# Two fp32 products in one kernel: where and when the sums of the weights' blocks are formed, split and stored in chunks 0 and 1

## The chip, the cores and the metric

The kernel runs on one core of a Trainium2 chip. The metric is the device time of one execution in microseconds. TensorE (PE) multiplies, VectorE (DVE) and GpSimd (POOL) do the element-wise work on two operands, ScalarE (ACT) the casts and the GELU. SyncE (SP) issues most DMAs in one fixed order, so that a DMA which has to wait for its data holds up every later one of that queue; a smaller queue of DMAs is issued by POOL between its own instructions.

## The reference

What the kernel computes, with 8 batches × 8 heads × 576 positions × 64:

```python
kv  = einsum('bhsd,bhse->bhde', k, v)
out = einsum('bhsd,bhde->bhse', q, kv)
rms = sqrt(mean(out * out, axis=-1, keepdims=True) + 1e-06)
x   = (out / rms * g_norm).transpose(0, 2, 1, 3).reshape(4608, 512)
h   = x @ w_in                              # 512 x 2048
g   = 0.5 * h * (1 + erf(h / sqrt(2)))
return (g @ w_out).astype(float32)          # 2048 x 512
```

## The kernel before, in words

The 4608 rows of `x` are worked in 9 chunks (`NCH`) of 512. To keep fp32 accuracy, each operand is held as a high half (a cast on ACT) and a low half (operand minus high half, on DVE), and a product of two operands is three matmuls: high·high, low·high, high·low. Between the two layers of a chunk the kernel forms the rows of the next chunk: `load_kv` and `sum_kv` for the keys and values, `scale` for the norm, `add_blocks` for sums of blocks.

**Chunk 0** is plain while the weights arrive. For each of the 16 blocks `i`, `layer1` (12 matmuls of 128x512) and `layer2` of block `i-1` (12 more) run, and `convert` turns the raw weights of two or three tiles into halves: `bits_w` (DVE, the `SCALAR_TENSOR_TENSOR` rows of L682), the low halves (DVE L695). The GELU's low half is `gl` (DVE L730). `bits_w` writes into two places, `x4` and `x5`, in turn.

**Chunk 1** (`FAST`) has a plain layer 1, and its layer 2 takes 7 block products in place of 8. It is worked in 28 steps, "ticks", of 12 matmuls of 128x256. Each tick's operand is made four ticks ahead by `ready` (high half ACT L1171, low half DVE L1172) from tiles that `combine` (L1161) adds up. **Chunks 2 to 8** do so in both layers.

The 7 products need sums of blocks of the weights, and these are formed once:

- `w_in` has eight pairs of tiles `j`. `sum_in(j)` adds four 128x256 blocks on DVE in chunk 0 (L581). For pairs 0 to 4 the sums go to DRAM from POOL's queue; in chunk 1 `load_sums` (SP L482) brings half a pair back, `high_sums` (ACT L487) and `low_sums` (DVE L491) split it, and `send(rounded)` has `product_out` (SP L417) write two 256 KB blocks to DRAM. For pairs 5 to 7 (`DIRECT = 5`), `split_in` does it at once in chunk 0: ACT casts into `x4` and `x5` (L429), DVE subtracts (L430), and POOL issues eight DMAs of 128 KB a pair out of those tiles (L437).
- `w_out`'s pairs: `sum_out(j)` does two 128x512 adds on DVE into `z`, then four 128x256 adds on POOL from `z` to `w` (L581 both). `split_out(j)` (ACT L995, DVE L996) writes the halves over the weights' own tiles, and `send(sent)` stores them.

The raw weights of chunk 1's layer 2 come by `load_raw` (SP L1025), and its first three, for the first ticks, stand at the end of layer 1 in SP's order. SBUF places that fall free are listed in `free` and handed out by `take`; the tile of weight `i` (`w_in{i}`) falls free when `layer1` has used it. In chunks 2 to 8 the sums come in through a ring of six tiles (`fetch`), but for those that stay (`RESIDENT`, `IN_PLACE`).

In chunk 1's layer 1 two PSUM banks (`h`) take the results in turn; ACT L1344 reads each. What stands behind it in an iteration is in this order:

```python
if i in SPLITS:
    split_out(SPLITS[i])
if i in SUMS_OUT:
    sum_out(SUMS_OUT[i])
```

Of the kernel before, what the change touches and what calls it, by code (L numbers as in the profile page):

```python
# [36 lines left out]
def linear_attn_rms_gelu_ffn(  # L37
# [371 lines left out]
    def product_out(at, src, eng=nc.sync):  # L409

        key, n = at[:-1], at[-1]
        if key in RAW_KEPT:
            to = resident_tile(key)[:, n * DM:(n + 1) * DM].rearrange("p (a n) -> p a n", a=2)
            eng.dma_start(out=to.bitcast(F32), in_=src.bitcast(F32))
            return
        to = product_of(key)[:, n * DM:(n + 1) * DM]
        eng.dma_start(out=to.rearrange("p (a n) -> p a n", a=2), in_=src.bitcast(F32))  # L417

    def product_of(key):
        if key not in products:  # L420
# [68 lines left out]
    def low_sums(j, second):  # L489
# [4 lines left out]
        t = t.rearrange("p (z k n) -> p k z n", z=2, k=2)  # L494
        rounded.extend(
            (place_in(j, k), t[:, a]) for a, k in enumerate((6, 5) if second else (1, 2))
        )
        rounded.append(name)
# [35 lines left out]
    def fetch(n):  # L534

        if n < len(queue):
# [938 lines left out]
```

## Time and profile before

| | |
|---|---|
| median of three runs | 799.0 us (798.01 to 800.65) |
| the profiled execution | 799.7 us, of which the span of instructions is 797.9 us |
| PE busy | 770.0 us (97% of the span) |
| DVE, ACT, POOL busy | 579.8, 392.6, 192.5 us |
| DMA | 253.84 MB, mean 318 GB/s |

Busy time is an average over all nine chunks; it says that PE has the most work, not where it stands still. In the rows below a piece such as `[6.65 <-DMA x]` is the idle time ahead of an instruction and what ended it; times are microseconds from the start of the span, and L numbers are those of the kernel before.

### The profile page before, as it was taken

The page shows a single profiled execution, that of the slowest core. Times are in us where ns is not written, and L with a number is a line of the kernel's source. Part 1 is how long each engine was busy: PE and PEld are TensorE (multiplying, and loading weights), DVE is VectorE, ACT ScalarE, POOL GpSimd, SP SyncE. Part 2 cuts the span into 40 slices and gives each one's busy share as a digit, 9 for nine tenths or more (in the row PEclk, how much of TensorE's full clock was granted, in tenths as well). Part 3 has the DMA queues.
Part 4 walks back from the last instruction along what each step waited for, and adds up shares of the span by engine and source line. Part 5 has one row for each costly group of instructions (what it writes and reads, how often), then busy time and mean ns, then how long its engine had stood idle before and what let it go on. Part 6 is the DMA issues. An engine that isn't in the chain of part 4 may idle for free.

```text
span 797.9 us, 17145 instructions
## 1 busy us (share of the span) xinstructions
PE 770.0 (97%) x6728; PEld 732.5 (92%) x6728; DVE 579.8 (73%) x1022; ACT 392.6 (49%) x760; POOL 192.5 (24%) x189
## 2 busy tenths in 40 slices
PE   9999599985999999999999999999999999999998
PEld 7888388764999999999999999999999999999998
DVE  3986676675965897589748974798489758975683
ACT  3997655642534453445444543454445444542361
POOL 1012323367101710071007200620071007101200
PEclk9999799997999999999999999999999999999999
DMA  9999987968699999799979997998899899789974
GB/s 348 407 413 400 370 281 259 314 201 277 208 307 348 336 350 406 259 332 358 406 266 330 345 399 283 326 337 301 295 330 333 297 314 324 277 279 362 327 277 143
DMA packets 98228, 253.84 MB, mean 318 GB/s; under 512 B 9572, under 2 KB 43876, under 8 KB 98148
## 3 DMA queue, kind: packets, MB, share of 16 engines
q1 hardware_dynamic: 96160, 246.98, 86.3%
q0 software_dynamic: 1984, 5.77, 1.9%
q8 instruction: 53, 0.87, 0.4%
q14 instruction: 27, 0.22, 0.1%
q10 hardware_dynamic: 4, 0.00, 0.0%
HBM read 214.43 MB, written 36.70 MB: 315 GB/s over the span
## 4 chain that ended last, share of the span: by engine, by line
PE 81%; ACT 6%; DMA 4%; DVE 3%; issue 3%; POOL 2%; SPq 0%; DVEq 0%; POOLq 0%; ACTq 0%
PE acc L1193 27%; PE acc L590 21%; PE h L590 13%; PE a L1193 11%; PE h L715 4%; PE acc L738 2%; ACT z L658 1%; POOL w L581 1%; PE acc L183 1%; ACT r L671 1%; DMA w_out<-w_out 1%; DMA w_in<-qT 1%; PE acc L237 1%; PE a L237 1%; DMA products_in<-x 1%
## 5 line engine op out<-in xcount | busy, mean ns | idle before, releaser
L590 PE MATMUL acc<-w_out,w_in 128*128 128x256 f32 x660 | 87.6, 276 | 0.0
L590 PEld LDWEIGHTS acc<-w_out,w_in 128*128 128x128 f32 x660 | 80.7, 188 | 0.0
L715 PE MATMUL h<-x,w_in 128*128 128x512 f32 x276 | 73.5, 392 | 0.0
L715 PEld LDWEIGHTS h<-x,w_in 128*128 128x128 f32 x276 | 51.6, 188 | 11.6 <-issue 0.6
L1193 PE MATMUL acc<-w_in,w_out 128*128 128x256 f32 x468 | 58.3, 276 | 0.0
L1193 PEld LDWEIGHTS acc<-w_in,w_out 128*128 128x128 f32 x468 | 55.5, 188 | 0.0
L590 PE MATMUL h<-w_out,w_in 128*128 128x256 f32 x396 | 53.6, 277 | 0.0
L1193 PE MATMUL acc<-w_in,w_in 128*128 128x256 f32 x408 | 50.7, 276 | 0.0
L590 PEld LDWEIGHTS h<-w_out,w_in 128*128 128x128 f32 x396 | 48.9, 188 | 0.5 <-issue 0.4
L1193 PEld LDWEIGHTS acc<-w_in,w_in 128*128 128x128 f32 x408 | 48.3, 188 | 0.0
L581 DVE TENSOR_TENSOR gl<-acc,gh 128x256 f32<-128x256 f32 (+1 forms) x78 | 34.7, 444 | 18.6 <-ACT gh L603 14.0
L738 PE MATMUL acc<-w_out,gh 128*128 128x512 f32 x128 | 42.9, 418 | 3.4 <-ACT gh L724 3.4
L590 PE MATMUL acc<-w_in,w_in 128*128 128x256 f32 x300 | 41.8, 276 | 0.0
L269 ACT ACTIVATE sq<-acc 128x512 f32<-128x512 f32 x14 | 8.4, 603 | 65.4 <-PE acc L237 65.4
L590 PEld LDWEIGHTS acc<-w_in,w_in 128*128 128x128 f32 x300 | 37.6, 188 | 0.0
L590 PE MATMUL acc<-s,w_in 128*128 128x256 f32 x270 | 37.1, 276 | 0.0
L279 DVE TRANSPOSE_TENSOR_REDUCE part<-sq 128x16 f32<-128x512 f32 x33 | 23.3, 707 | 17.8 <-ACT sq L269 17.8
L622 ACT ACTIVATE w_out<-acc 128x512 f32<-128x512 f32 x33 | 19.8, 599 | 33.4 <-DVE acc L581 33.4
L1193 PE MATMUL acc<-w_out,w_in 128*128 128x256 f32 x282 | 35.6, 278 | 0.0
L738 PEld LDWEIGHTS acc<-w_out,gh 128*128 128x128 f32 x128 | 25.8, 203 | 9.8 <-ACT gh L724 4.3
L715 PE MATMUL h<-s,w_in 128*128 128x512 f32 x96 | 30.2, 396 | 4.4 <-ACT w_in L1344 2.9
L1193 PEld LDWEIGHTS acc<-w_out,w_in 128*128 128x128 f32 x282 | 33.9, 188 | 0.1
(362 smaller groups left out, 1966.9 us busy)
## 6 DMA issues: line engine op xcount, KB each, us to landing
w_in<-products_in SPq DMA_DIRECT2D x172, 512.0 KB, 5.2
w_in<-products_out SPq DMA_DIRECT2D x142, 512.0 KB, 5.4
products_in<-w_in SPq DMA_DIRECT2D x42, 256.0 KB, 5.7
products_out<-w_out SPq DMA_DIRECT2D x38, 256.0 KB, 5.1
w_in<-w_in SPq DMA_DIRECT2D x16, 512.0 KB, 11.6
w_out<-w_out SPq DMA_DIRECT2D x16, 512.0 KB, 11.3
q<-qT SPq DMA_DIRECT2D x15, 512.0 KB, 7.1
kv_main<-kv_main SPq DMA_DIRECT2D x14, 512.0 KB, 8.3
```

The source lines that it names most:

```text
L183: nc.tensor.matmul(out=ps[r, n * D:(n + 1) * D], lhsT=k[:, r], rhs=v[:, r], start=(j == 0), stop=(j == NJ),)
L237: nc.tensor.matmul(out=ps[rows(h), p % 2 * HALF + a:p % 2 * HALF + e], lhsT=kv[b % 2][rows(half), p, h ^ half], rhs=q[rows(half), h, a:e], ...
L269: nc.scalar.activation(out=sq, in_=ps, func=AF.Square)
L279: nc.vector.tensor_reduce(out=self.part[:, 2 * k[0] + k[1], :], in_=sq.rearrange("p (b d) -> p b d", d=BLK), op=ALU.add, axis=AX.X, apply_ ...
L581: return eng.tensor_tensor(out=out, in0=x, in1=y, op=op)
L590: nc.tensor.matmul(out=out, lhsT=y, rhs=x[:, z, kb], start=first and kb + i == 0, stop=kb == 1 and i == 2, skip_group_check=True,)
L622: nc.scalar.activation(out=grid(t)[:, :, j % 2], in_=ps.rearrange("p (a n) -> p a n", a=2), func=AF.Gelu)
L658: nc.scalar.activation(out=zs[n].bitcast(F32), in_=top.bitcast(F32), func=AF.Prelu, scale=2.0 ** -112, alpha=2.0 ** 32,)
L671: nc.scalar.activation(out=tails[n], in_=raw[n].bitcast(mybir.dt.uint8).rearrange("p (n b) -> p n b", b=8)[:, :, 3], func=AF.Copy, scale=1 ...
L715: nc.tensor.matmul(out=h, lhsT=parts["in", i][:, w][:, p * P:(p + 1) * P], rhs=at.x[p][:, x], start=(m + p == 0), stop=(m == 2 and p == NP ...
L738: nc.tensor.matmul(out=ps, lhsT=x[:, ts], rhs=parts["out", i][:, w], start=(i == 0 and m == 0), stop=(m == 2 and (i == NF - 1 or (i, t) == ...
L1193: nc.tensor.matmul(out=self.bank[name][a][:, a * HALF:(a + 1) * HALF], lhsT=x[:, at], rhs=y, start=(k in (0, 2, 1) and n + p + m == 0 and ...
```

## The change

1. `split_in`, `DIRECT` and `pending` are gone. All eight pairs of `w_in` send their sums to DRAM in chunk 0, and the halves of pairs 5 to 7 are loaded, split and written in chunk 1: 11 halves in layer 1 (`LOAD`, split three iterations after the load, before two), five in layer 2 (`LATE`, split four ticks after).
2. `sum_out` adds in place, in one pair of tiles (`SPOTS`) in place of two. Pairs 0 to 3 are summed in chunk 0 (`SUMS_0`), two of them split there (`SPLITS_0`); pairs 4 to 7 follow in chunk 1.
3. `layer1` in chunk 1 uses four PSUM banks in turn: `h0`, `h1`, `acc0`, `acc1`.
4. Chunk 0's `scale` moves from DVE to POOL, one of its `split_x` from POOL to DVE. Chunk 1's `scale` uses the work tiles `gh`, `gl`, not a place of `free`.
5. `load_kv(3, ...)`'s last two stand at iterations 8 and 10 (before 10 and 12), `raw_out(6)` and `(7)` at 5 and 6 (before both at 0). `take` hands out the place that has been free longest. The four resident loads are spread over chunk 2's start (`KEEP`), and of `w_out`'s sums (6,2) stays in place of (1,2).

```diff
-    pending = []
-    def split_in(j, s, first):
-        for t, hi in zip(s, first):
-            nc.scalar.copy(out=hi.bitcast(F32R), in_=t)
-            nc.vector.tensor_tensor(
-                out=t.bitcast(F32R), in0=t, in1=hi, op=ALU.subtract
-            )
-        for z, parts_z in enumerate((first, s)):
-            for n, k in enumerate((1, 2, 6, 5)):
...
-                nc.gpsimd.dma_start(
-                    out=to, in_=parts_z[n // 2][:, n % 2 * HALF:(n % 2 + 1) * HALF]
-                )
-    DIRECT = 5
...
-        if direct:
-            pending.append((j, s, (a, b)))
-            return
...
     def load_sums(j, second):
-        name, t = take(F32R, first=SHORT)
+        n = 2 * j + second
+        if n < len(KEPT_RAW):
+            name, t = KEPT_RAW[n], block_tile(KEPT_RAW[n], F32R)[:, :2 * DM]
+        else:
+            name, t = take(F32R, first=RINGS if n >= LATE[3] else SHORT)
...
-    IN_PLACE = [(k, GROUPS - 1) for k in (1, 2, 6, 5)] + [(1, 2), (2, 2)]
+    IN_PLACE = [(k, GROUPS - 1) for k in (1, 2, 6, 5)] + [(2, 2), (6, 2)]
...
-        name = next(n for n in [*(n for n in first if n in free), *free]
+        name = next(n for n in [*(n for n in free if n in first), *free]
...
-        h = next_bank("h")
+        h = bank(f"acc{i % 2}") if at.c and i % 4 > 1 else next_bank("h")
...
-            if 12 <= i < 15:
-                for n in ((0,), (1, 2), (3,))[i - 12]:
-                    nxt.scale(n)
+            if 11 <= i < 15:
+                nxt.scale(i - 11, nc.gpsimd)
             if i in (13, 14):
-                nxt.split_x(i - 13)
+                nxt.split_x(i - 13, nc.vector if i == 13 else nc.gpsimd)
...
-    halves = [(j, second) for j in range(DIRECT) for second in range(2)]
+    halves = [(j, second) for j in range(NJ2) for second in range(2)]
...
+    SPOTS = {0: "x5", 1: "x5", 2: "w", 3: "z", 4: "w", 5: "z", 6: "w", 7: "z"}
-    def sum_out(j):
+    def sum_out(j, eng=nc.gpsimd):
...
-        for o, x, op, y in (
-            (s1, a21, ALU.add, a22), (s2, s1, ALU.subtract, a11),
-            (s3, a11, ALU.subtract, a21), (s4, a12, ALU.subtract, s2),
-        ):
-            add(o, x, y, op, nc.gpsimd)
-        wide[j] = s
+        add(a22, a21, a22, eng=eng)
+        add(a21, a11, a21, ALU.subtract, eng)
+        add(a11, a22, a11, ALU.subtract, eng)
+        add(a12, a12, a11, ALU.subtract, eng)
+        wide[j] = w
...
+    SUMS_0 = {12: 0, 13: 1, 14: 2, 15: 3}
+    SPLITS_0 = {13: 0, 14: 1}
...
+                send(rounded)
+                if i in LATE:
+                    load_sums(*halves[LATE[i]])
+                if i - 4 in LATE:
+                    high_sums(*halves[LATE[i - 4]])
+                    low_sums(*halves[LATE[i - 4]])
...
-    SUMS_OUT = {0: 1, 2: 2, 4: 3, 5: 4, 7: 5, 9: 6, 11: 7}
-    SPLITS = {0: 0, 2: 1, 4: 2, 5: 3, 7: 4, 9: 5, 11: 6, 13: 7}
-    LOAD = {1: 1, 2: 2, 4: 3, 5: 4, 6: 5, 8: 6, 9: 7, 11: 8, 12: 9}
+    SUMS_OUT = {1: 4, 3: 5, 5: 6, 7: 7}
+    SPLITS = {0: 2, 1: 3, 3: 4, 5: 5, 7: 6, 9: 7}
+    LOAD = {-1: 0, 0: 1, 1: 2, 2: 3, 3: 4, 4: 5, 5: 6, 6: 7, 7: 8, 9: 9, 11: 10}
+    LATE = {3: 11, 5: 12, 7: 13, 9: 14, 11: 15}
+    KEEP = {(0, False): (0, 1), (2, False): (2,), (4, False): (3,)}
...
-        if i in (10, 12):
-            load_kv(3, i // 2 - 3)
+        if i in (8, 10):
+            load_kv(3, i // 2 - 2)
```

DVE's order in chunk 0, around block `i = 7` (`x5_415` and `x4_454` are the two places `x5`, `x4`; `w_908`, `w_909` the sums of pair 5). Before:

```order
L581 TENSOR_TENSOR w_909<-x5_415,w_908 128x256
L682 SCALAR_TENSOR_TENSOR x5_415<-z_903,r0_336 128x512
L730 TENSOR_TENSOR gl_950<-h1_936,gh_949 128x512
L695 TENSOR_TENSOR w_in11_953<-x4_454,w_in11_953 128x512
L430 TENSOR_TENSOR w_908<-w_908,x5_415 128x512
L430 TENSOR_TENSOR w_909<-w_909,x4_454 128x512
L682 SCALAR_TENSOR_TENSOR x5_415<-z_955,r0_336 128x512
L695 TENSOR_TENSOR w_out10_977<-x5_415,w_out10_977 128x512
```

and of the change, whose L567, L668, L716 and L681 are the L581, L682, L730 and L695 of before:

```order
L567 TENSOR_TENSOR w_909<-x5_415,w_908 128x256
L668 SCALAR_TENSOR_TENSOR x5_415<-z_903,r0_336 128x512
L716 TENSOR_TENSOR gl_954<-h1_940,gh_953 128x512
L681 TENSOR_TENSOR w_in11_957<-x4_454,w_in11_957 128x512
L668 SCALAR_TENSOR_TENSOR x5_415<-z_959,r0_336 128x512
L681 TENSOR_TENSOR w_out10_965<-x5_415,w_out10_965 128x512
```

The two L430 are gone, and the next write to `x5` no longer stands behind a cast and four DMAs that read it. The same holds for the two later pairs.

SP's order at the end of chunk 1's layer 1. Before (`sums_4_1` is the second half of pair 4, the last that is loaded):

```order
L482 DMA w_in11_1976<-sums_4_1_821 128x512
L137 DMA w_in7_1978<-kv_main 128x1024
L159 DMA w_in8_1915<-kv_tail 128x256
L1025 DMA w_in12_1981<-products_out_0_0_782 128x1024
L1025 DMA w_in13_2008<-products_out_0_1_930 128x1024
L417 DMA products_in_4_0_1233<-w_in10_1952 128x2x256
L417 DMA products_in_4_1_1237<-w_in10_1952 128x2x256
L1025 DMA w_in14_2033<-products_out_0_2_1106 128x1024
```

and of the change (L470, L1008, L426 are L482, L1025, L417 of before):

```order
L137 DMA w_in9_1904<-kv_main 128x1024
L159 DMA w_in3_1848<-kv_tail 128x256
L426 DMA products_in_4_0_1216<-w_in6_1823 128x2x256
L426 DMA products_in_4_1_1220<-w_in6_1823 128x2x256
L470 DMA w_in10_1926<-sums_5_0_914 128x512
L1008 DMA w_in6_1950<-products_out_0_0_782 128x1024
L426 DMA products_in_2_3_1965<-w_in8_1878 128x2x256
L426 DMA products_in_4_2_1218<-w_in8_1878 128x2x256
L1008 DMA w_in12_1974<-products_out_0_1_934 128x1024
L1008 DMA w_in8_1997<-products_out_0_2_1082 128x1024
```

The kv loads now stand ahead of pair 4's last writes. Two of the three raw loads (L1008) go into `w_in6` and `w_in8`, out of which the two writes just ahead of each still read.

POOL's order from chunk 0's end on. Before, behind the 24 L437 (the first four rows are the last of those; then chunk 0's `split_x`, then `sum_out(0)` of chunk 1):

```order
L437 DMA products_in_0_1267<-w 128x256
L437 DMA products_in_1_1269<-w 128x256
L437 DMA products_in_3_1081<-w 128x256
L437 DMA products_in_2_1272<-w 128x256
L348 TENSOR_TENSOR s_1363<-o,s_1363 128x512
L348 TENSOR_TENSOR s_1413<-o,s_1413 128x512
L581 TENSOR_TENSOR w<-z 128x256
L581 TENSOR_TENSOR w<-w,z 128x256
```

and of the change, where the first six rows stand in chunk 0:

```order
L330 TENSOR_TENSOR o<-o,sq 128x512 x2
L567 TENSOR_TENSOR x_415<-x_415 128x256 x4
L330 TENSOR_TENSOR o<-o,sq 128x512
L567 TENSOR_TENSOR x_415<-x_415 128x256 x4
L330 TENSOR_TENSOR o<-o,sq 128x512
L348 TENSOR_TENSOR s_1400<-o,s_1400 128x512
L567 TENSOR_TENSOR w<-w 128x256 x4
L567 TENSOR_TENSOR z<-z 128x256 x4
```

In place of DMA issues POOL has four `scale` and two `sum_out` in chunk 0; six `sum_out` follow, in `w` and `z` in turn.

## Rows read from the trace of the kernel before

**Rows 1.** Waits of PE: line, what it waited for, us in total, times, longest.

```profile
PE acc L183 <- DMA w_in<-kv_main: 6.6, 1, 6.6
PE acc L738 <- DVE gl L730: 6.0, 1, 6.0
PE acc L738 <- ACT gh L724: 3.4, 1, 3.4
PE h L715 <- ACT w_in L1344: 2.9, 2, 1.7
PE h L715 <- ACT s L1344: 1.5, 1, 1.5
```

**Rows 2.** Windows by stage: stretch, length, busy PE, PEld, DVE, ACT, POOL, clock, DMA share, GB/s.

```profile
60.00:77.40 17.40, 17.40 (x96) 14.21 (x95) 12.40 (x24) 14.71 (x27) 4.85 (x9) 1.00 1.05 401
77.40:103.30 25.90, 16.51 (x50) 11.89 (x49) 15.87 (x29) 16.23 (x32) 7.01 (x13) 0.74 1.04 361
103.30:127.90 24.60, 24.60 (x177) 20.17 (x176) 19.67 (x36) 11.42 (x22) 6.90 (x10) 1.00 0.76 257
127.90:182.10 54.20, 49.80 (x255) 39.43 (x253) 37.52 (x56) 27.37 (x52) 28.08 (x32) 1.00 0.78 254
182.10:202.60 20.50, 11.54 (x117) 10.36 (x117) 12.26 (x12) 7.07 (x14) 16.86 (x14) 0.67 0.84 285
202.60:237.80 35.20, 35.20 (x306) 34.94 (x304) 28.09 (x46) 17.14 (x31) 0.00 (x0) 1.00 0.80 275
237.80:797.90 560.10, 556.79 (x5281) 553.21 (x5280) 410.36 (x736) 252.07 (x496) 123.15 (x90) 1.00 0.89 319
```

**Rows 3.** Timeline of chunk 0's stall: start, us, engine, line, operation, idle time before.

```profile
80.63 0.69 DVE L682 SCALAR_TENSOR_TENSOR x<-z,r 128x512 int32<-128x512 int32 x1 [6.65 <-DMA products_in<-x]
...
97.57 0.69 DVE L682 SCALAR_TENSOR_TENSOR x<-z,r 128x512 int32<-128x512 int32 x1 [5.16 <-DMA products_in<-x]
```

**Rows 4.** Chain that ended last, 77 to 128 us: start, us, what.

```profile
108.73 2.48 PE a L183 x80
...
116.95 2.74 PE h L715 x12
119.70 2.80 PE acc L738 x12
```

**Rows 5.** DMA issues: tile, queue, count, KB each, us from issue to landing.

```profile
w_in<-sums SPq DMA_DIRECT2D x9, 256.0 KB, 3.5
...
products_in<-x POOLq DMA_DIRECT2D x12, 128.0 KB, 6.7
```

**Rows 6.** Timeline of layer 2's start in chunk 1, 176 to 206 us.

```profile
195.86 0.62 ACT L1171 CAST w_in<-s 128x512 fp32r<-128x512 f32 x1 [6.77 <-DMA products_in<-w_in]
```

**Rows 7.** SP's queue: waits of 100 to 240 us, as in rows 1.

```profile
SPq L159 <- POOL o L330: 8.2, 1, 8.2
```

**Rows 8.** Window inside chunk 1's layer 2, columns as in rows 2.

```profile
204.00:216.00 12.00, 12.00 (x107) 12.00 (x106) 11.96 (x21) 7.18 (x14) 0.00 (x0) 1.00 0.65 238
```

**Rows 9.** Chain that ended last, 180 to 240 us: a write of sums, and one tick.

```profile
193.87 4.88 DMA products_in<-w_in
...
205.80 1.37 PE a L1193 x12
```

**Rows 10.** Timeline of POOL and DVE in chunk 1, 104 to 206 us.

```profile
129.94 0.73 POOL L581 TENSOR_TENSOR w<-z 128x256 f32<-128x256 f32 x1 [6.70 <-DVE z L581]
...
175.16 5.46 POOL L330 TENSOR_TENSOR o<-o,w_in 128x512 f32<-128x512 f32 x4
...
183.15 0.73 POOL L581 TENSOR_TENSOR w<-z 128x256 f32<-128x256 f32 x1 [2.52 <-DVE z L581]
...
190.01 1.75 DVE L1172 TENSOR_TENSOR w_in<-x,w_in 128x512 fp32r<-128x512 f32 x1
...
203.41 0.68 DVE L1172 TENSOR_TENSOR w_in<-w_in,w_in 128x512 fp32r<-128x512 f32 x1
```

More of the change, by code (lines that the diff above doesn't have):

```diff
@@ L400, in linear_attn_rms_gelu_ffn, with product_of, product_of_key @@
     products = {}
+    def product_of(key):
+        if key not in products:
+            products[key] = dram.tile([P, 2, DM], F32, name="_".join(map(str, ("products", *key))))
+        return products[key]
+    def product_of_key(key):
+        return product_of(key).rearrange("p a n -> p (a n)")
     def resident_tile(key):
@@ L493, in low_sums @@
         )
[L494 to L498, printed above, removed]
+        rounded.append(([place_in(j, k) for k in ((6, 5) if second else (1, 2))], by_place(t)))
+        if name not in KEPT_RAW:
+            rounded.append(name)
     ORDER = (0, 2, 4, 6, 1, 3, 5)
@@ L543, in fetch @@
             ring[n] = kept[i][:, away:away + 2 * DM]
-            nc.sync.dma_start(out=ring[n].bitcast(F32), in_=products[key])
+            nc.sync.dma_start(out=ring[n].bitcast(F32), in_=product_of_key(key))
     def aligned(c, key):
@@ L1021, in load_raw @@
         away = AWAY if k == 3 else 0
-        name = next(x for x in [*first, *SHORT, *free] if x in free)
+        name = next(x for x in [*first, *(x for x in free if x in SHORT), *free] if x in free)
         free.remove(name)
         t = block_tile(name, F32R)[:, away:away + 2 * DM]
-        nc.sync.dma_start(out=t.bitcast(F32), in_=products["out", k, n])
+        nc.sync.dma_start(out=t.bitcast(F32), in_=product_of_key(("out", k, n)))
         raws[FAST, k, n] = name, t
@@ L1045, in op_tile @@
         shifted = n == GROUPS - 1 or k == 3 or (k, n) in IN_PLACE
-        names = [x for x in (SHORT if i < 17 else KEPT_IN) if x in free]
+        names = [x for x in free if x in RINGS and i < 17] + [x for x in free if x in KEPT_IN]
         if shifted or not names:
-            return take(F32R, True)
+            return take(F32R, i >= 17, [x for x in PLACES if x not in SHORT])
         free.remove(names[0])
@@ L1128, in linear_attn_rms_gelu_ffn @@
             load_w(BEHIND[i])
+        if i in SPLITS_0:
+            split_out(SPLITS_0[i])
+        if i in SUMS_0:
+            sum_out(SUMS_0[i])
         if i == 15:
@@ L1131, in linear_attn_rms_gelu_ffn @@
             load_sums(*halves[0])
-            sum_out(0)
+            send(sent)
     class Fast:
@@ L1370, in linear_attn_rms_gelu_ffn @@
         if i in (9, 10):
-            if i == 9:
-                names["spread"], spread = take(first=SHORT)
-            for n in range(2):
-                nxt.scale(
-                    (0, 2, 1, 3)[2 * (i - 9) + n], nc.gpsimd, spread[:, n * CH:(n + 1) * CH]
-                )
-            if i == 10:
-                free.append(names.pop("spread"))
+            for n, name in enumerate(("gh", "gl")):
+                spread = work.tile([P, CH], F32, name=name, bufs=2)
+                nxt.scale((0, 2, 1, 3)[2 * (i - 9) + n], nc.gpsimd, spread)
         if i in (11, 12):
@@ L1407, in linear_attn_rms_gelu_ffn @@
         before_layer1(c)
-        if c == FAST + 1:
-            for key in RESIDENT[:NJ2 // 2]:
-                keep(key)
         for j, second in parts_of_layer1():
+            if c == FAST + 1:
+                for n in KEEP.get((j, second), ()):
+                    keep(RESIDENT[n])
             if not second:
```

82 lines of the change are left out of this document (34 added, 48 removed).

## The prediction

> **What bounds the kernel now.** I read the waits of PE first [rows 1]: there are few, and they are long. The windows by stage then say where they fall [rows 2]. Chunks 2 to 8, the last of the windows, keep PE busy for 556.79 of 560.10 us: nothing to gain there. The loss stands in three places ahead of them.
>
> *Chunk 0, 77.4 to 103.3 us.* The window is 25.90 us long and holds 50 matmuls, two blocks' worth. A block at full pace takes 2.74 + 2.80 us [rows 4], so two take 11.1, and 14.8 us are lost: PE waits 3.4 and 6.0 us for the GELU's halves [rows 1], and the rest is shorter idle time and a clock of 0.74 in that window. The reason is one step further back. DVE stands 6.65 and 5.16 us ahead of a `bits_w` [rows 3], since the place that it writes is still read by POOL's DMAs of `split_in`, which take 6.7 us to land [rows 5]. DVE's queue is in order, so `gl` waits behind it.
>
> *Chunk 1's layer 1.* PE waits 2.9 + 1.5 = 4.4 us for ACT to read a result bank [rows 1]. PE is busy 49.80 of 54.20 us, which agrees.
>
> *The start of chunk 1's layer 2, 182.1 to 202.6 us.* The window of 20.5 us holds 117 matmuls: the 80 of a kv sum (2.48 us [rows 4]) and three ticks (1.37 us each [rows 9]), 6.6 us of work. So 13.9 are lost. SP's queue had stood for 8.2 us with a load of the keys' tail, until POOL's `scale` had released its place [rows 7]; PE then waited 6.6 us for the keys [rows 1], and the first operands' casts waited 6.77 us for writes of `w_in`'s sums to leave their tiles [rows 6].
>
> **The change part by part.** The sum is made against the profiled execution, 799.7 us, which lies 0.7 over the median of 799.0.
>
> *`split_in` goes.* With no L430 and no cast into `x4`, `x5`, nothing reads the two places but DVE itself, and both long waits of `bits_w` lose their reason: 14.8 us, if nothing takes their place. Two things can. ACT was busy 14.71 of 17.40 us in the window before the stall, when PE ran through [rows 2], so the GELU there has little slack, but six casts go. And the DMAs: 361 GB/s × 25.9 us + 257 × 24.6 are 15.7 MB from 77.4 to 127.9 us; the change takes away 24 writes of 128 KB and adds 6 of 256, so 14.1 MB have to pass in 50.5 - 14.8 = 35.7 us, 395 GB/s. The rows show 401 in one window and 361 in another; at 361 it takes 39.1 us, 3.4 too long. Bounds 0 and 3.4 us given back; I take 1.5, about the middle. Term: **-13.3**.
>
> *Four pairs of `sum_out` in chunk 0, `scale` to POOL.* DVE gains six adds of 128x512, four low halves and a `split_x`, and loses six L430 and four `scale`: about even at 0.69 us each, and it was busy 19.67 of 24.60 us at the chunk's end [rows 2]. POOL, busy 6.90 us of the same window, gains two rounds of four adds (3 us each at 0.73) and four `scale` (5.46 us [rows 10]), and has room for these 11.5. ACT, 11.42 of 24.60, takes four casts. Nothing. If that cover were gone, the `gl` of blocks 14 and 15 would be late, by at most the net one instruction, 0.7 us.
>
> *Four banks.* The three bank waits of 4.4 us go: a layer-1 block takes 2.74 us, so ACT may be two blocks late where it could be one, and the longest wait was 1.7 [rows 1]. Term: **-4.4**; the lower bound is 0, if ACT itself falls behind.
>
> *Keys earlier, no place taken by `scale`.* SP's wait of 8.2 us and PE's of 6.6 behind it go with the place that caused them. Term for the window's whole loss: **-13.9**.
>
> *What SP must carry.* This is what takes a part back. Let T be the start of chunk 1's layer 1. Without waits the fourth tick could start at T + 49.8 + 2.5 + 4.1 = T + 56.4. Up to pair 4's last writes, SP's order of the change holds 63 units of 256 KB (a 512 KB load counts as two). One unit takes 0.73 us at 361 GB/s and 0.80 at the 254 GB/s by a share of 0.78 of chunk 1 [rows 2]; I take 0.76, so 47.9 us. The DMAs of chunk 0 come over late by up to 3.4 - 1.5 = 1.9, I take 1.0. Then come three round trips in a row, in which a place is written out and used again: `w_in6` and `w_in8`, into which raw loads go, and `w_in10`, the operand tile of the fourth tick. The first ends behind a full queue, 4.9 us [rows 9]; the next two find it drained, and I take 3.5 each, as loads of sums take [rows 5], with 1.5 us for the two writes before each. The operand's cast and low half add 1.3. Fourth tick: T + 1.0 + 47.9 + 4.9 + 1.5 + 3.5 + 1.5 + 3.5 + 1.3 = T + 65.1, 8.7 later than it could be. Term: **+8.7**. If the queue keeps up and the trips lie beside other work, 0; with 0.80 a unit, 1.9 late and 4.9 for every trip, T + 71.3, so +14.9.
>
> *Five halves in layer 2.* Five low halves of 0.68 us [rows 10] are 3.4 us on a DVE that was busy 11.96 of 12.00 us there [rows 8]. Operands are made four ticks ahead, 5.5 us, which hides most: **+1.0**, bounds 0 and 3.4.
>
> *The places' order, the ring's residents, the spread of the four resident loads, raw products at later iterations.* As many bytes as before, in chunks whose PE has 3.3 us idle in 560 [rows 2]; the cover is the ring's six tiles of lead. Nothing; if it is gone, rival D.
>
> Sum: 799.7 - 13.3 - 4.4 - 13.9 + 8.7 + 1.0 = 777.8; less the 0.7 by which the profiled execution lies above the median, **777.1 us**.
>
> **A rule that speaks against it.** A low half on DVE took 0.68 us with POOL idle and 1.75 beside POOL's adds [rows 10]: two engines that get in each other's way. The Trainium skill ("SBUF — State Buffer", "SBUF: two separate sides") says that a DVE instruction with two SBUF operands and a POOL instruction that reads SBUF exclude each other for a whole instruction, which agrees in direction. By it POOL's rounds stretch with every DVE addition that stands beside them, and the time would be rival C's 783.7; by the rows alone, whose spacing of rounds holds such meetings already, it is 777.1.
>
> **The rivals.**
>
> *A, the forecast:* SP's queue sets the start of layer 2. 772 to 783 us. For it: three places written and used again in a row of the queue. Chance 0.50.
>
> *B, the queue keeps up:* no 8.7. 777.1 - 8.7 = 768.4, and 766 if chunk 0 gives all back as well. For it: the DMA share of chunk 1 is only 0.78, and the queue stood for 8.2 us of it [rows 2, 7]. Against it: the three round trips follow one another in an ordered queue, whatever its rate. Chance 0.20.
>
> *C, POOL's chain is late:* `sum_out`'s rounds followed each other every (183.15 - 129.94) / 7 = 7.6 us [rows 10], though one is 3 us of POOL. Six of them, then `scale` (5.46 us) and the block sums, come before the operands that POOL adds up for the first ticks. At 7.6 us a round they are in time; at 8.7, slowed by DVE's denser adds, they end 6.6 us later, SP's writes and the operands with them: 777.1 + 6.6 = 783.7, range 781 to 790. Against it: two rounds fewer than before stand in chunk 1. Chance 0.19.
>
> *D, slower:* with (6,2) in place of (1,2) and the later resident loads a ring tile is needed before it is there, in each of chunks 2 to 8. From 24.3 / 7 = 3.5 us a chunk on it eats the gain: 802 us or more at 3.6. Against it: PE waits for no DMA there [rows 1], the bytes are the same. Chance 0.04.
>
> *E, chunk 0 stalls anyway:* `split_in` went, but the loads, at a share of 1.04 there [rows 2], are what DVE waits for: no 13.3, 790.4 us. Against it: the waits name POOL's writes [rows 3]. Chance 0.05. That the losses all come back elsewhere, so that the time is as before: 0.02.
>
> **How the numbers follow.** The prediction is A's, 777.1; its own range is 772 to 783. B reaches down to 766, C up to 790. Low 765.5 and high 788 leave out E, D, no change, and C's upper part, about 0.15. A measurement of this kernel can tell about 0.3% from no change, 2.4 us. Faster by more: A, B, C, E, 0.94; same 0.02; slower D, 0.04.
>
> **What would show it.** Right: no wait of `bits_w` for `products_in<-x`, and blocks of 5.5 us from 62 us to T, which stands near 114 us. No wait of `h` for ACT in chunk 1. Keys ahead of their sum. At the first four ticks PE waits for raw loads, or an operand's cast for `products_in`, some 9 us in all, with SP's queue waiting for writes ahead of L1008; a DMA share near 1 in chunk 1. Chunk 2 begins near 216 us in place of 237.8, and 560 us follow, as before. Wrong: no such waits (B); waits for POOL's L567, or SP behind `w_out`'s low halves (C); waits for `products` in chunks 2 to 8 (D); `bits_w` waiting for `w_in` or `w_out` loads (E).

## The result, and the profile after

The changed kernel takes 787.84 us (median of four, 785.6 to 790.72) against 798.66 before: a ratio of 0.9862, 95% interval 0.9825 to 0.9899. Forecast were 777.1 us and a range of 765.5 to 788. So it is faster by 1.4%, half of what was forecast; the median lies 0.16 us under the upper end of the range, and two of the four executions (788.05 and 790.72) lie above it. The profiled execution took 787.62 us, its span 785.9.

The windows by stage, cut at the same events as [rows 2] (columns as there):

```profile
60.00:77.30 17.30, 17.30 (x96) 14.11 (x89) 15.21 (x29) 17.22 (x33) 2.17 (x4) 1.00 1.05 402
77.30:102.00 24.70, 24.70 (x178) 20.34 (x177) 20.26 (x41) 13.73 (x28) 9.93 (x14) 1.00 1.02 361
102.00:115.90 13.90, 11.86 (x49) 8.78 (x48) 8.36 (x14) 7.10 (x14) 6.33 (x7) 1.00 1.06 367
115.90:125.60 9.70, 6.91 (x25) 4.27 (x24) 9.57 (x11) 4.95 (x10) 7.60 (x7) 1.00 0.79 281
125.60:169.50 43.90, 43.41 (x229) 35.17 (x228) 30.35 (x47) 24.68 (x48) 22.45 (x24) 1.00 0.92 297
169.50:186.70 17.20, 8.77 (x117) 8.14 (x116) 6.93 (x8) 4.67 (x10) 14.65 (x11) 0.80 0.87 275
186.70:225.80 39.10, 36.98 (x300) 36.47 (x301) 31.14 (x51) 20.51 (x38) 0.00 (x0) 0.96 0.87 319
225.80:785.90 560.10, 556.82 (x5281) 553.24 (x5280) 410.20 (x736) 252.00 (x496) 123.02 (x90) 1.00 0.89 321
```

The stall of chunk 0 is gone: PE is busy for all of the second row. A new loss stands at the seam of the chunks (third and fourth row): 7.0 us without PE's or below its pace, since two blocks of 5.5 us and one more fill 23.6 us. The start of layer 2 lasts 17.2 us, before 20.5; its other ticks 39.1, before 35.2. Chunks 2 to 8 take 560.1 us in both kernels, to a tenth. Layer 2 of chunk 1 ends 12.0 us earlier, and that is the whole gain of the profiled execution.

The waits of PE, as in [rows 1]:

```profile
PE a L1181 <- DMA w_in<-products_out: 6.0, 2, 5.0
PE acc L1181 <- DMA w_in<-products_out: 1.9, 1, 1.9
PE acc L1181 <- ACT w_in L1159: 1.6, 1, 1.6
PE acc L724 <- DVE w_out L681: 1.4, 2, 0.9
PE h L701 <- ACT x L343: 1.3, 1, 1.3
...
PE h L701 <- DVE x L348: 1.0, 2, 0.6
PE acc L183 <- DMA w_in<-kv_main: 0.8, 1, 0.8
PE acc L724 <- ACT gh L710: 0.6, 1, 0.6
PE h L701 <- ACT w_in L1340: 0.5, 1, 0.5
PE acc L724 <- DVE gl L716: 0.5, 1, 0.5
```

Of the 20.4 us of waits in [rows 1] 2.4 are left: 0.8 for the keys, 0.6 and 0.5 for the GELU's halves (L710, L716 are the L724, L730 of before) and 0.5 for a bank. Raw loads (`w_in<-products_out`) and the seam's `split_x` (L343, L348) took the place of the others. The timeline of ACT, DVE and POOL at the seam shows why:

```profile
103.80 0.66 ACT L644 ACTIVATE z<-w_out 128x512 f32<-128x512 f32 x1 [10.94 <-DMA w_out<-w_out]
...
111.49 3.95 POOL L567 TENSOR_TENSOR x<-x 128x256 f32<-128x256 f32 x4 [2.43 <-DVE x L567]
115.39 1.75 POOL L330 TENSOR_TENSOR o<-o,sq 128x512 f32<-128x512 f32 x1
...
117.17 1.17 ACT L343 CAST x<-o 128x512 fp32r<-128x512 f32 x2 [1.07 <-POOL o L330]
...
117.61 2.37 DVE L567 TENSOR_TENSOR w<-w_out 128x512 f32<-128x512 f32 x2
119.90 1.82 DVE L348 TENSOR_TENSOR x<-o,x 128x512 fp32r<-128x512 f32 x2
```

ACT stands 10.9 us for the last raw weight; `split_x` needs the last `scale` (L330), which stands behind a pair's four adds on POOL, and on DVE it stands behind two adds of the next pair, which take 1.2 us each beside POOL and 0.68 alone (128 to 160 us).

At the start of layer 2, the chain that ended last goes three times through a write of sums, as the forecast had it:

```profile
168.12 5.84 DMA products_in<-w_in
174.02 0.33 SPq L1008
...
174.88 4.42 DMA products_in<-w_in
179.37 0.33 SPq L1008
...
180.23 5.71 DMA products_in<-w_in
186.04 0.63 ACT w_in L1159
...
209.26 6.38 DMA w_in<-products_out
```

### The profile page after: what moved, and what is told of

Read it like the earlier page. It is cut to its first block, busy times and chain, and to the rows that moved or that the text cites. A ratio compares the mean times of both kernels' runs of the same rounds, so it can differ in the third digit from the quotient of the medians.

```text
span 785.9 us, 17145 instructions
## 1 busy us (share of the span) xinstructions
PE 764.9 (97%) x6728; PEld 728.7 (93%) x6728; DVE 575.7 (73%) x1019; ACT 391.7 (50%) x760; POOL 191.8 (24%) x174
## 4 chain that ended last, share of the span: by engine, by line
PE 75%; DMA 4%; DVE 3%; issue 1%; SPq 1%; POOL 0%; ACT 0%; DVEq 0%; ACTq 0%; POOLq 0%
PE acc L1181 25%; PE acc L576 21%; PE h L576 13%; PE a L1181 10%; DMA products_in<-w_in 3%; PE acc L183 1%; PE h L701 1%; PE acc L701 1%; PE acc L237 1%; DMA w_in<-products_out 1%; PE a L237 1%; DMA w_in<-sums 1%; DVE w_in L1160 0%; SPq L426 0%; POOL w L567 0%
## 5 line engine op out<-in xcount | busy, mean ns | idle before, releaser
L701 PE MATMUL h<-x,w_in 128*128 128x512 f32 x228 | 59.4, 394 | 2.3 <-ACT x L343 1.3
L1181 PE MATMUL acc<-w_in,w_out 128*128 128x256 f32 x498 | 61.5, 276 | 0.0
L1181 PEld LDWEIGHTS acc<-w_in,w_out 128*128 128x128 f32 x498 | 58.8, 188 | 0.0
L701 PEld LDWEIGHTS h<-x,w_in 128*128 128x128 f32 x228 | 42.5, 188 | 13.2 <-ACT x L343 2.1
L567 DVE TENSOR_TENSOR gl<-acc,gh 128x256 f32<-128x256 f32 (+1 forms) x78 | 34.6, 444 | 18.6 <-ACT gh L589 14.0
L724 PE MATMUL acc<-w_out,gh 128*128 128x512 f32 x128 | 40.3, 394 | 2.0 <-DVE w_out L681 1.4
L576 PE MATMUL acc<-w_in,w_in 128*128 128x256 f32 x270 | 37.9, 276 | 0.0
L279 DVE TRANSPOSE_TENSOR_REDUCE part<-sq 128x16 f32<-128x512 f32 x33 | 23.3, 707 | 17.2 <-ACT sq L269 17.1
L576 PEld LDWEIGHTS acc<-w_in,w_in 128*128 128x128 f32 x270 | 33.9, 188 | 0.0
L576 PEld LDWEIGHTS acc<-s,w_in 128*128 128x128 f32 x270 | 33.2, 188 | 0.0
L1149 POOL TENSOR_TENSOR w_in<-w_in,w_in 128x512 f32<-128x512 f32 x3 | 4.3, 1440 | 116.3 <-ACT w_in L608 116.3
L1181 PE MATMUL acc<-w_out,w_out 128*128 128x256 f32 x258 | 32.4, 276 | 0.0
L1181 PE MATMUL a<-w_in,w_in 128*128 128x256 f32 x198 | 26.4, 287 | 6.0 <-DMA w_in<-products_out 6.0
L724 PEld LDWEIGHTS acc<-w_out,gh 128*128 128x128 f32 x128 | 23.9, 188 | 8.3 <-DVE w_out L681 2.3
```

Source lines behind the costliest of these rows:

```text
L279: nc.vector.tensor_reduce(out=self.part[:, 2 * k[0] + k[1], :], in_=sq.rearrange("p (b d) -> p b d", d=BLK), op=ALU.add, axis=AX.X, apply_ ...
L567: return eng.tensor_tensor(out=out, in0=x, in1=y, op=op)
L576: nc.tensor.matmul(out=out, lhsT=y, rhs=x[:, z, kb], start=first and kb + i == 0, stop=kb == 1 and i == 2, skip_group_check=True,)
L701: nc.tensor.matmul(out=h, lhsT=parts["in", i][:, w][:, p * P:(p + 1) * P], rhs=at.x[p][:, x], start=(m + p == 0), stop=(m == 2 and p == NP ...
L724: nc.tensor.matmul(out=ps, lhsT=x[:, ts], rhs=parts["out", i][:, w], start=(i == 0 and m == 0), stop=(m == 2 and (i == NF - 1 or (i, t) == ...
L1149: eng.tensor_tensor(out=out, in0=x, in1=y, op=op)
```

## The experiments

Each edit is made to the changed kernel where nothing else is said. Layer 1 and layer 2 are those of chunk 1; the times are read from PE's rows in the profiled execution, in us: starts, and for layer 1's end the end of its last matmul, up to 0.1 us behind the start of the kv sum at which the windows are cut.

| run | layer 1 | its end | fourth tick | end of layer 2 | median of runs |
|---|---|---|---|---|---|
| before | 127.87 | 182.1 | 202.6 | 237.8 | 798.66 |
| changed | 115.94 | 169.6 | 186.7 | 225.8 | 787.84 |
| two_banks | 116.46 | 176.9 | 187.3 | 227.0 | 791.38 |
| early_load | 113.06 | 166.3 | 182.3 | 222.0 | 785.85 |
| raw_first | 115.11 | 170.3 | 187.4 | 224.7 | 789.60 |
| other_places | 115.18 | 170.2 | 185.4 | 224.1 | 787.64 |
| direct_back | 131.23 | 185.0 | 199.9 | 234.8 | 795.60 |
| sums_late | 114.50 | 170.2 | 187.6 | 230.0 | 793.89 |
| scale_dve | 116.70 | 170.3 | 187.4 | 225.8 | 788.73 |
| seam_sums | 115.65 | 169.1 | 187.0 | 226.9 | 787.68 |
| joined | 113.46 | 168.0 | 180.9 | 222.8 | 783.06 |
| joined_seam | 113.08 | 164.7 | 177.7 | 219.5 | 781.31 |
| keys_early (on before) | 127.93 | 182.2 | 198.8 | 235.2 | 796.76 |

Medians of four runs scatter by some 2 us (the last section has a possible reason), so what tells the theories apart is mostly the stage times.

**direct_back: `split_in` back for pairs 5 to 7.**

```diff
...
+        if j >= DIRECT:
+            pending.append((j, s, (a, b)))
+            return
...
+        if j < DIRECT:
             nc.sync.dma_start(out=t[:, LO].bitcast(F32), in_=sums_in[j, second])
...
```

> The change, but pairs 5 to 7 of w_in's sums are split and written in chunk 0 by split_in, as before (chunk 1 takes and frees the same places for these six halves, without their loads, splits and writes). Theory M (split_in's DMAs out of x4 and x5 were chunk 0's loss, and the forecast's 13.3 us are theirs): the waits of bits_w for products_in come back, 5 to 7 us each, PE loses 11 to 15 us in chunk 0, chunk 1's layer 1 begins at 127 to 131 us in place of 115.9; layer 2 from the fourth tick on gets 1 to 3 us shorter (no late halves); the time is 794 to 800 us. Rival W (the weights' last loads would have set chunk 0's pace anyway): layer 1 of chunk 1 begins before 121 us and the time is 788 to 791.

Theory M holds: the ratio to before is 0.9966 (0.9956 to 0.9977), and DVE's waits are back, where [rows 3] has them. Layer 1 begins at 131.2 us, just behind the 127 to 131 expected. The ticks from the fourth on take 34.9 us in place of 39.1, all of it PE's; that is more than the 1 to 3 us expected. The timeline of DVE and a window:

```profile
79.39 0.69 DVE L688 SCALAR_TENSOR_TENSOR x<-z,r 128x512 int32<-128x512 int32 x1 [5.71 <-DMA products_in<-x]
...
96.07 0.69 DVE L688 SCALAR_TENSOR_TENSOR x<-z,r 128x512 int32<-128x512 int32 x1 [4.91 <-DMA products_in<-x]
```

```profile
199.90:234.80 34.90, 34.90 (x305) 34.77 (x304) 27.25 (x44) 17.07 (x31) 0.46 (x1) 1.00 0.77 274
```

So taking `split_in` away brings 131.23 - 115.94 = 15.3 us in chunk 0 and costs 4.2 us in layer 2's ticks, and 2.2 at its start (17.2 us in place of 15.0). The 4.2 us are of two kinds. The fourth and fifth ticks take 5.0 us in the changed kernel and 2.8 here: behind the changed kernel's waits the granted clock is lower there, 0.60 in the mean of this window, so for most of it at the lower of its two levels (1.2 and 2.4 GHz):

```profile
187.40:191.70 4.30, 4.26 (x23) 4.26 (x24) 4.27 (x8) 3.02 (x6) 0.00 (x0) 0.60 1.03 410
```

From the sixth tick on the changed kernel takes 34.1 us and direct_back 32.1; of these 2.1, 1.9 are the changed kernel's wait for a raw load.

**sums_late: `w_out`'s sums in place, but when the kernel before forms them.**

```diff
...
-    SUMS_0 = {12: 0, 13: 1, 14: 2, 15: 3}
-    SPLITS_0 = {13: 0, 14: 1}
+    SUMS_0 = {15: 0}
+    SPLITS_0 = {}
...
```

> The change, with w_out's sums in place, but summed and split when the kernel before does it: pair 0 in block 15 of chunk 0, the seven others in chunk 1. Theory G (four sums and two splits in chunk 0's last four blocks, on DVE, POOL and ACT, are what makes split_x and the GELU late at the seam): PE's waits for split_x go from 2.3 us to under 0.7, chunk 1's second block begins 2 to 4 us earlier than 125.6; what is gained is given back when POOL's longer row of sums, scale and block sums ends after 186 us, and the time is 787 to 791 us. Rival S (the load of w_out15 alone makes the seam): the second block begins within 1.5 us of 125.6, and the time is 789 us or more.

Theory G holds for the seam: layer 1's first block, with chunk 0's last part of layer 2, takes 5.5 us (114.50 to 120.04), all PE's, in place of 9.7 in the changed kernel (fourth row of its windows). The second block begins 5.6 us earlier, more than the 2 to 4 expected. The window below runs 0.2 us into it:

```profile
114.50:120.20 5.70, 5.70 (x26) 4.66 (x25) 2.93 (x5) 1.70 (x4) 2.46 (x4) 1.00 0.59 203
```

All of it and more is given back. PE waits 3.7 us for ACT at 159 us, and POOL's last sum for an operand starts at 191.1 us, in the changed kernel at 183.3. The time, 793.89 us (791.83 to 795.84, ratio 0.9944), is longer than the 787 to 791 expected: the pairs in chunk 0 are worth 4 us at the end of layer 2 and some 6 in the median although they cost 5.6 at the seam. The timeline of ACT, DVE and POOL at layer 2's start:

```profile
180.42 1.72 POOL L365 TENSOR_TENSOR w<-z,o 128x512 f32<-128x512 f32 x1
180.93 1.76 DVE L1160 TENSOR_TENSOR w_in<-w_in,w_in 128x512 fp32r<-128x512 f32 x1
...
186.91 0.62 ACT L1159 CAST w_in<-s 128x512 fp32r<-128x512 f32 x1 [6.67 <-POOL s L1149]
...
191.11 1.61 POOL L1149 TENSOR_TENSOR r<-r 128x512 f32<-128x512 f32 x1
```

A low half that takes 0.69 us with POOL idle takes 1.76 here, and POOL's sums 1.6 to 1.7 in place of 1.27. The Trainium skill ("SBUF — State Buffer", "SBUF: two separate sides") has a DVE instruction with two SBUF operands and a POOL instruction that reads SBUF exclude each other for a whole instruction; the trace, with both durations longer, agrees with its direction. The cast of the fourth tick's operand stands 6.67 us for POOL. That is rival C, and it is what sums formed late meet; in the changed kernel the same cast stands 9.00 us (186.04) for a write of `w_in`'s sums, and POOL had done its sum by 179.

**early_load: the last raw weight one iteration earlier.**

```diff
-    BEHIND = {6: weights.index(("in", NF - 1)), 10: weights.index(("out", NF - 1))}
+    BEHIND = {6: weights.index(("in", NF - 1)), 9: weights.index(("out", NF - 1))}
```

> The change, but the raw load of the last w_out tile (w_out15) is issued one iteration earlier in chunk 0, ahead of six writes of products in SP's order. Theory S (at the seam of chunks 0 and 1, 102 to 125.6 us, ACT stands 10.9 us for this load, GELU, gl, scale and split_x wait behind it in their engines' order, and PE loses 7 us there): ACT's wait falls under 4 us, PE's waits at the seam fall from about 5 us to under 2, and chunk 1's second block begins at 120 to 122 us in place of 125.6. The end then depends on whether SP's queue moves along: 783 to 786 us if it does. Rival P (POOL's sums and scale in chunk 0 are what makes split_x late, whatever ACT does): the waits for split_x stay over 2 us and the time within 1 us of 787.8.

Theory S holds in part. ACT's wait is 6.12 us, not under 4; layer 1 begins 2.9 us earlier and its second block at 122.4 us, a little later than the 120 to 122 expected. The first block still takes 9.4 us: PE still waits 1.5 us there for `split_x` and what follows it on DVE, and the granted clock of the block is 0.82. So the load made the blocks ahead of layer 1 late, the sums the one behind its start. The queue moved along: the fourth tick is 4.4 us earlier. Median 785.85 us (ratio 0.9832, 0.9795 to 0.987), at the upper end of 783 to 786. ACT's row:

```profile
98.97 0.68 ACT L644 ACTIVATE z<-w_out 128x512 f32<-128x512 f32 x1 [6.12 <-DMA w_out<-w_out]
```

**scale_dve and seam_sums: two other edits at the seam.**

```diff
-                nxt.scale(i - 11, nc.gpsimd)
+                nxt.scale(i - 11, nc.vector)
```

> The change, but chunk 0's four scale instructions on DVE, not on POOL. Theory P (scale stands behind sum_out's four adds in POOL's order, and split_x behind scale): PE's waits for split_x, 2.3 us with ACT's and DVE's share, fall under 1 us, and the second block of chunk 1 begins 1 to 2.5 us earlier; the end moves by less, since SP's queue sets the start of layer 2: 785 to 788 us. Rival V (DVE, which gets four instructions of 0.69 us more, is just as late): the waits stay, within 1 us of 787.8.

Rival V holds: the waits for `split_x` become 0.64 and 1.22 us, 1.9 in place of 2.3; the first block takes 9.6 us, the stages stay, and the time is 788.73 us.

```diff
-    SUMS_0 = {12: 0, 13: 1, 14: 2, 15: 3}
-    SUMS_OUT = {1: 4, 3: 5, 5: 6, 7: 7}
+    SUMS_0 = {12: 0, 13: 1, 15: 2}
+    SUMS_OUT = {0: 3, 1: 4, 3: 5, 5: 6, 7: 7}
```

> The change, but pair 2 of w_out's sums is formed in block 15 of chunk 0, behind split_x in DVE's order, and pair 3 in block 0 of chunk 1. Theory G (the sums on DVE and POOL ahead of split_x cost 4 us in chunk 1's first block): that block takes 6.5 to 8 us in place of 9.9, layer 1 ends at 166.5 to 168.5 us in place of 169.6, and the time is 785 to 787 us. Rival P (a pair more in chunk 1 makes POOL's row of sums end later, as with all sums late): layer 1 ends within 0.7 us of 169.6 or the fourth tick starts at 186 us or later, and the time is 787 us or more.

The first block takes 8.0 us in place of 9.7, as theory G has it. But PE waits 1.6 us for ACT at 160.6, layer 1 ends 0.5 us earlier and the fourth tick starts at 187.0: what follows is rival P's. The time is that of the change.

**two_banks: layer 1 with two result banks.**

```diff
-        h = bank(f"acc{i % 2}") if at.c and i % 4 > 1 else next_bank("h")
+        h = next_bank("h")
```

> The change, but with two result banks in chunk 1's layer 1 as before. Theory Q (SP's queue and its three round trips set the start of chunk 1's layer 2): the three waits of PE for ACT come back, 3 to 4.4 us in layer 1, but the fourth tick starts when the queue lets it, near 186.7 us as in the changed kernel, so the wait for the first raw load shrinks from 5.0 us to 1 or 2 and the time stays at 787 to 789 us. Rival B4 (the banks' gain reaches the end): the start of layer 2 moves back with layer 1, and the time is 791 to 792 us.

By the stages theory Q holds. Layer 1 takes 60.4 us in place of 53.6, with waits of 2.0 and 2.1 us and a clock of 0.94; and the fourth tick starts 0.6 us later, 0.5 of which stood at layer 1's start already, and layer 2 ends 1.2 later. The median, 791.38 us (786.44 to 792.95), would have been the rival's; but its profiled execution, 792.95, loses 4 us of PE's pace in chunks 2 to 8 (last section), so the time does not decide. The timeline of PE:

```profile
154.63 0.73 PE L701 MATMUL h<-s,w_in 128*128 128x512 f32 x2 [2.00 <-ACT r L1340]
161.37 0.72 PE L701 MATMUL h<-s,w_in 128*128 128x512 f32 x2 [2.14 <-ACT w_in L1340]
...
179.29 1.68 PE L1181 MATMUL a<-w_in,w_in 128*128 128x256 f32 x12
```

The 5.0 us wait ahead of the first tick is gone: the banks' gain turns into a wait for the queue.

**other_places: the first raw loads into places without a round trip.**

```diff
-        name = next(x for x in [*first, *(x for x in free if x in SHORT), *free] if x in free)
+        latest = [x for x in free if x in SHORT]
+        if k == 0:
+            latest.reverse()
+        name = next(x for x in [*first, *latest, *free] if x in free)
```

> The change, but the first three raw loads of chunk 1's layer 2 go into w_in12 to w_in14, free since layer 1 used them, in place of w_in6, w_in12, w_in8; operand tiles of the second and third tick then use w_in6 and w_in10. Theory Q (round trips of places written out and used again set the start): SP's queue no longer stands 4 to 5 us ahead of a raw load, the first tick starts near 173 us in place of 178, the fourth at 181 to 183 in place of 186.7, and the time is 783 to 785 us. Rival C (POOL's block sums, which end at 184.6 us, are the next bound): the first ticks move but the fourth to sixth do not start before 185, and the time falls by less than 2 us.

Neither theory holds as put. SP no longer stands ahead of the raw loads, and issues the first at 169.8 in place of 174.0; but that load now takes 7.7 us, and the first tick starts at 177.65, 0.4 us earlier. The fourth starts at 185.4 and the time stays, as rival C has it, but not for its reason: the fourth tick starts before POOL's last sum ends (185.5), and ahead of the third an operand's cast stands for a write, not for POOL. So one round trip is left, that of the operand's place. The chain, and ACT's row:

```profile
169.83 7.68 DMA w_in<-products_out
...
177.65 4.40 PE a L1184 x24
...
182.72 0.62 ACT L1162 CAST w_in<-r 128x512 fp32r<-128x512 f32 x1 [4.83 <-DMA products_in<-w_in]
```

The DMA share is 0.99 from 155 to 185 us. So behind the two trips that went lie the third and the rate of the queue; the run does not part them.

**raw_first: in layer 2, raw loads ahead of the late halves' writes.**

```diff
+                for at in RAWS.get(i, ()):
+                    load_raw(*at)
                 send(rounded)
...
-                for at in RAWS.get(i, ()):
-                    load_raw(*at)
```

> The change, but in chunk 1's layer 2 a tick's raw loads stand ahead of that tick's writes of split sums in SP's order, not behind. Theory L (five late halves' writes hold up the raw loads of product 3, for which PE waits 1.9 us at 215.8, and stands at a low clock after it): the wait goes, layer 2 takes 37 us from the fourth tick on in place of 39.1, and the time falls by 1.5 to 2.5 us, to 785.3 to 786.3. Rival D (DVE, busy throughout from 195.8 to 213.7 us, is what makes these ticks late): PE's wait moves to DVE's low halves and the time falls by less than 0.7 us.

The ticks from the fourth on take 37.3 us in place of 39.1, near the 37 of theory L, but the gain does not lie where the theory has it. The fourth and fifth ticks take 3.4 us in place of 5.0, since the lower granted clock falls ahead of them here (0.83 from 182.0 to 187.4 us, 1.00 behind). From the sixth on it is 33.9 us in place of 34.1: the wait of 1.9 us comes back as waits of 0.5 and 0.8 for raw loads. The changed kernel's clock reads 1.00 behind its wait at 215.8, so the low clock that the expectation has there is not seen. The time, 789.60 us (788.02 to 792.05), is longer than the change's; the profiled execution took 2.8 us more from the end of layer 2 on, though nothing there was edited, in a stretch of slower pace (last section). So theory L is shown neither by the stages nor by the time, and rival D's reason is not seen either, as the waits are for loads.

**keys_early: on the kernel before, the earlier keys and the spread without a taken place alone.**

```diff
...
-        if i in (10, 12):
-            load_kv(3, i // 2 - 3)
+        if i in (8, 10):
+            load_kv(3, i // 2 - 2)
```

> The kernel before, with one part of the change alone: load_kv(3, 2) and (3, 3) at iterations 8 and 10 of chunk 1, and chunk 1's scale spreading into gh and gl in place of a taken place. Theory K (SP's stand of 8.2 us behind the keys' tail, and PE's 6.6 us for the keys, are most of the 13.9 us lost at the start of layer 2): the fourth tick starts at 64 to 68 us after layer 1's start in place of 74.7, and the time is 790 to 793 us. Rival W (the casts that wait 6.77 us for writes out of w_in10 and w_in11 keep the start where it is): the keys' wait goes, the fourth tick moves by less than 3 us, 796 us or more.

This is nearer to rival W. The waits for the keys are gone, the fourth tick starts 3.8 us earlier, 70.9 after layer 1's start where theory K has 64 to 68, and the time is 796.76 us (ratio 0.998, 0.9969 to 0.9992): 1.9 us of gain where the forecast has 13.9 less 8.7. Each of the first ticks now waits for its operand. The timeline of PE, and ACT's row behind it:

```profile
187.17 0.50 PE L1193 MATMUL a<-w_in,w_in 128*128 128x256 f32 x2 [2.50 <-ACT w_in L1171]
189.91 2.93 PE L1193 MATMUL a<-w_in,w_in 128*128 128x256 f32 x12 [2.24 <-DVE w_in L1172]
```

```profile
195.04 0.62 ACT L1171 CAST w_in<-w_in 128x512 fp32r<-128x512 f32 x1 [5.90 <-DMA products_in<-w_in]
```

**joined and joined_seam: several edits together.** `joined` has the edits of early_load and raw_first, first raw loads that prefer free places outside the ring (an edit that its expectation does not name), and half 10 moved into layer 2; `joined_seam` adds that of seam_sums.

```diff
...
-    LOAD = {-1: 0, 0: 1, 1: 2, 2: 3, 3: 4, 4: 5, 5: 6, 6: 7, 7: 8, 9: 9, 11: 10}
-    LATE = {3: 11, 5: 12, 7: 13, 9: 14, 11: 15}
+    LOAD = {-1: 0, 0: 1, 1: 2, 2: 3, 3: 4, 4: 5, 5: 6, 6: 7, 7: 8, 9: 9}
+    LATE = {1: 10, 3: 11, 5: 12, 7: 13, 9: 14, 11: 15}
```

> The change with three edits: w_out15's load one iteration earlier, a tick's raw loads ahead of its writes, and the last half of layer 1's loads (the first of pair 5) moved into layer 2, so that w_in10 takes the first raw load without a round trip and the first operand tiles are w_in11 to w_in15. Theory Q: chunk 1's layer 1 begins at 113 us as with the early load alone; the first tick waits under 2 us in place of 5, the fourth starts at 176 to 179 us, layer 2 ends at 214 to 217 and the time is 776 to 780 us. Rival R (the rate of the DMAs, not the round trips, sets the start, since the queue is full when the raw loads are issued): the fourth tick starts at 181 us or later and the time is 782 to 785 us.

> The joined kernel (early load, raw loads first, half 10 in layer 2) with pairs 2 and 3 of w_out's sums one block later, as in the run seam_sums. Theory G: chunk 1's first block takes 6.5 to 8 us in place of 10.8, and the time falls from 783.1 to 780 to 782. Rival R (the rate of the DMAs sets the start of layer 2, so that a shorter layer 1 only waits longer): the fourth tick stays within 1 us of 180.9 and the time within 1 us of 783.

`joined` takes 783.06 us (ratio 0.9799, 0.9766 to 0.9832): its first tick waits 2.5 us, not under 2, its fourth starts at 180.9, 0.1 us short of rival R's 181 or later, and the time is rival R's. `joined_seam` takes 781.31 us (781.06 to 781.38, ratio 0.9782, 0.9767 to 0.9797), 6.5 us under the change and the fastest here: its first block takes 6.2 us, and the fourth tick moves along by 3.2. Here R fails, as SP's queue moved along too: it issues the first raw load at 164.1 us, in `joined` at 166.9. Its windows from layer 1 on:

```profile
113.08:164.70 51.62, 49.68 (x255) 39.52 (x255) 35.27 (x55) 29.01 (x56) 26.28 (x29) 1.00 0.99 332
164.70:177.70 13.00, 8.84 (x116) 8.15 (x117) 6.88 (x7) 4.72 (x10) 12.61 (x10) 0.87 0.93 320
177.70:219.40 41.70, 37.17 (x302) 35.37 (x300) 32.67 (x51) 20.61 (x39) 2.24 (x2) 1.00 0.83 283
```

A DMA share of 0.99 through layer 1 leaves little room for more transfers there; the 41.7 us of the ticks, 6.8 above those of direct_back, are now the largest loss.

## Why the forecast was half right

The direction, the mechanism of rival A and chunks 2 to 8 were right; four stages came out longer than forecast. That the time lies in the range at all is luck, by 0.16 us: 787.84 us is outside A's own 772 to 783 and inside C's 781 to 790. What speaks for A is not the number but the trace (three round trips in the chain, and a write, not POOL, ahead of the fourth tick's cast) and two_banks. Against the sum of 777.8 the profiled execution has 787.6, 9.8 more:

| stage | forecast | measured | off by |
|---|---|---|---|
| layer 1 begins | 114.6 (127.9 - 13.3) | 115.9 | 1.3 |
| layer 1 | 49.8 (54.2 - 4.4) | 53.6 | 3.8 |
| kv sum and three ticks | 15.3 (6.6 + 8.7) | 17.2 | 1.9 |
| the other ticks | 36.2 (35.2 + 1.0) | 39.1 | 2.9 |

- **`split_in`, -13.3.** This was right, and by its reason: direct_back shows 15.3. What came instead was not the ACT or the DMAs in general, but one load, the last raw weight: layer 1 begins 2.9 us earlier when it is issued earlier.
- **"Nothing" for the sums and `scale` in chunk 0.** This step failed. Cover was counted by busy shares (DVE 19.67 of 24.60 us [rows 2]), the cost came from order: `split_x` stands behind `scale`, that behind four adds on POOL, and behind two adds on DVE, which are slower beside POOL. The price of the sums is 5.6 us by the start of layer 1's second block (sums_late), 4.2 of it in one block (9.7 against 5.5), where the text had at most 0.7. `scale` alone costs nothing that scale_dve shows.
- **Four banks, -4.4.** In layer 1 they bring more, 6.8 us (two_banks). At the fourth tick 0.6 of it is left. The step was added to the sum as if it were independent of the queue; where the queue sets the next start, an earlier end of layer 1 is only waited off.
- **-13.9 and +8.7.** The three round trips stand where the text put them, but the fourth tick came at T + 70.8, not T + 65.1. The trips take 5.8, 4.4 and 5.7 us in place of 4.9, 3.5 and 3.5, which is 4.1 more: the queue was not drained, the DMA share was 0.87. And the queue reached the first of them at T + 52.2, not T + 48.9; the steps between and behind the trips were 1.7 shorter. The text had the queue carry its units without a stand, but from T to there SP stands 5.0 us at one time for `w_out`'s low halves and 4.2 for those of `w_in`'s sums:

```profile
SPq L426 <- DVE w_out L980: 5.2, 2, 5.0
...
SPq L426 <- DVE x L479: 4.4, 2, 4.2
```

  The first of these lies at the seam: these low halves, at 125 us, stand behind the late `split_x` and a pair's adds in DVE's order. In early_load it is gone, and there the fourth tick comes earlier by more than layer 1 does. The keys were the last wait of several: alone they bring 3.8 us at the fourth tick (keys_early).
- **Late halves, +1.0.** From the sixth tick on they cost 2.1 us (direct_back), and 1.9 of these are a wait for a raw load that the text did not have. That their writes stand ahead of the raw loads in SP's order is not the cause by itself: raw_first puts the loads ahead of their tick's writes and gains 0.2. The rest of the 2.9 us in the table lies in the fourth and fifth ticks, at the lower clock behind the waits of layer 2's start.
- **The rivals.** B fell with the round trips (its 766 is 766.9 by the text's own terms), D with 560.1 us in both kernels. C did not decide here, but does in sums_late. How much of layer 2's start is trips and how much is the DMAs' rate is not settled: other_places took away two trips of three, and the loads became longer.

## What to carry to other kernels

Price moved work by what stands behind it in the order of its engine up to the next instruction that PE waits for, not by the engine's idle share. When an in-order DMA queue sets the start of the next stage, gains ahead of that start do not add up (two_banks) unless they move the queue along as well (early_load, joined_seam). So work the queue's order through once: count each stand for another engine's data, and each place that is written out and used again as a round trip at the loaded latency of that stretch. And in front of late work, look for the loads that PE then waits for.

## What the runs showed of the hardware

In some executions PE has stretches of some 35 or 76 us in chunks 2 to 8 in which the same matmuls follow each other 4% more slowly, at a granted clock that reads 1.00 all the same. The chain of two_banks has both paces, for 192 equal matmuls of two chunks (117.8 and 113.3 ns each), and the windows of the two stretches have the clock (the third number from the end, as in [rows 2]):

```profile
286.69 22.61 PE acc L1181 x192
...
368.43 21.76 PE acc L1181 x192
```

```profile
286.69:309.30 22.61, 22.61 (x196) 22.48 (x198) 15.44 (x26) 9.22 (x17) 0.00 (x0) 1.00 1.03 390
368.43:390.19 21.76, 21.76 (x197) 21.63 (x198) 15.82 (x27) 9.33 (x17) 0.00 (x0) 1.00 1.03 405
```

They begin and end at different places in different executions. By the starts of its matmuls two_banks has them from 274 to 309 and from 675 to 751 us, raw_first from 671 to 748, and the changed kernel none behind layer 2 of chunk 1. At 4%, 111 us are some 4 us and 76 us some 3: the sizes by which two_banks (564.2 us) and raw_first (562.9) take longer than the changed kernel (560.1) from that point on. Only profiled executions show the pace; how much of the scatter between executions of one kernel (up to 7.6 us, other_places) such stretches make is not shown. What sets them off stays open.
